# Output products of the MoE stage issued in groups, with four gated blocks kept

## The chip, the cores and the metric

One Trainium2 chip, one of its cores. The metric is device time in microseconds (us), lower is better: the median of several executions of one launch. The core has a matrix engine (TensorE, PE in the rows), with its own row for weight loads (PEld), a vector engine (DVE), an activation engine (ACT), a general engine (POOL) and a queue engine that issues most transfers (SP). PSUM is the memory that TensorE writes to; it has eight banks here, one per accumulator.

## The reference, cut to what matters

```python
# q, k, v: 8 batches x 8 heads x 576 rows x 64 columns
k_p = k.reshape(B, H, 72, 8, D).mean(axis=3)      # v_p likewise
attn = softmax(q @ k_p.T / sqrt(D))               # 72 pooled keys
x = (attn @ v_p), heads joined                    # 4608 tokens x 512
a = x @ w1;  b = x @ w2                           # 512 x 1024 each
out = ((a * b) @ w3) @ w_out                      # 4608 x 512
```

## The kernel before

All numbers are float32, and every large product is made in three passes: a value is split into a rounded part and a rest (`hi`, `lo`), and hi*hi, hi*lo and lo*hi are added in PSUM. The kernel first makes W = w3 @ w_out once (lines 639 to 650). The tokens then go through in 12 chunks (m = 0 to 11) of 384. For a chunk, the 1024 gated columns are eight blocks (j = 0 to 7) of 128, and for each block:

- `a_mm m j` and `b_mm m j` (line 562): twelve matmuls each, 384 columns wide, into PSUM bank `a` and into PSUM bank `b`. There is one bank of each.
- `a_post` (line 572, ACT) copies bank `a` to SBUF; `g_mul` (line 580, DVE) multiplies it with bank `b`. So the next `a_mm` waits for `a_post`, and the next `b_mm` for `g_mul`.
- `g_hi` (line 585, ACT) and `g_lo` (line 591, DVE) split the gated block into `gh` and `gl`. There are two buffers of each.
- `out_mm m j` (line 607): nine matmuls, 512 columns wide, that add the block's share to the banks `o0`, `o1` and `o2`. After the eighth block of a chunk, `out_post` copies these out and SP stores them.

Beside this the attention of a later chunk n is made: `tr_q` (DVE), `s_mm` (line 434, the scores, in four banks of which one is bank `a` up to chunk 6 and bank `b` from 7 on), `soft_max`, `soft_sub`, `soft_exp`, `soft_sum`, `soft2` (lines 446 to 478, mostly DVE), `pt_turn` (line 510, DVE, into the one tile `T`), `pt_move` (line 517, four transfers on SP, out of `T`), `av_mm` (line 535, which uses bank `a` too), `x_hi` and `x_lo` (lines 543 and 546). `pt_turn` of the next part waits until `pt_move` has emptied `T`. POOL sums the pooled keys and values in trees of three adds (lines 381 to 386).

What each engine does next is written out by hand in the string `ORDER`: each engine takes its instructions in that order and none overtakes another on its engine. The entries `at(...)` only make the list of steps that `ORDER` names. The 12 entries of `out_mm` per chunk need only stand behind their `g_lo`, and before the chunk's `out_post`.

Of the kernel before, what the change touches and what calls it, by code (L numbers as in the profile page):

```python
# [19 lines left out]
def kernel(  # L20
# [768 lines left out]
    for m in range(NCH):  # L789
        m0 = M0 + 3 * NJ * m  # L790
        for j in range(NJ):
            k = m0 + 3 * j
# [4 lines left out]
            at("P", k + 2, g_hi, m, j)
            at("P", k + 2.5, g_lo, m, j)
            at("M", k + 5 + ([1.5, 0.0][j] if m >= JOINT - 1 and j < 2 else 0), out_mm, m, j)
        if m < NCH - 1:  # L800
            for t in range(3):
                at("P", m0 + 3 * NJ + 3, out_post, m, t)
    for n in range(1, NCH):
# [4 lines left out]
        else:  # L808
            av = k + (16 if n < JOINT - 1 else 7.5 if n < JOINT else 4.4)
            k -= 0 if n < JOINT - 1 else {JOINT - 1: 5, JOINT: 13}.get(n, 17.5)  # L810
# [8 lines left out]
    for b in range(1, B):  # L819
# [89 lines left out]
        a_post 1 0; g_mul 1 0; prep_k 2 0; prep_k 2 2; out_mm 0 7; out_post 0 0; g_hi 1 0; soft_exp 2 0 1;
        load_q 3 (3,); a_mm 1 1; a_post 1 1; prep_k 2 3; out_post 0 2; soft_max 2 1 1 1; b_mm 1 1; tr_q 3 0;  # L910
        soft_sum 2 0 0; soft_sub 2 1 1 1; load_q 3 (2,); soft_sum 2 0 1; soft2 2 0; a_mm 1 2; pt_turn 2 0;
        g_mul 1 1; g_lo 1 0; out_post 0 1; b_mm 1 2; prep_v 2 0; warm 0; prep_k 2 1; out_mm 1 0;
        soft_sub 2 1 0 1; soft_exp 2 1 0; a_post 1 2; a_mm 1 3; soft_max 2 2 0 0; soft_sub 2 2 0 0; g_hi 1 1;
        g_lo 1 1; pt_move 2 0; soft_sum 2 1 0; out_mm 1 1; soft_max 2 1 1 0; b_mm 1 3; soft_exp 2 2 0;
        soft_sub 2 1 1 0; soft_exp 2 1 1; a_post 1 3; soft_sum 2 1 1; soft2 2 1; pt_turn 2 1; g_mul 1 2;
        a_mm 1 4; g_hi 1 2; g_lo 1 2; b_mm 1 4; soft_max 2 2 1 0; soft_sub 2 2 1 0; soft_exp 2 2 1; pt_move 2 1;
        load_q 3 (1,); out_mm 1 2; prep_k 3 0; soft_sum 2 2 0; g_mul 1 3; load_k 3 3; a_mm 1 5; soft_sum 2 2 1;
        tr_q 3 3; soft2 2 2; prep_k 3 3; load_v 2 1; tr_q 3 1; pt_turn 2 2; g_hi 1 3; g_lo 1 3; a_post 1 4;
        pt_move 2 2; kt_mm 2; tr_q 3 2; load_v 2 2; kt_post 2; g_mul 1 4; b_mm 1 5; a_post 1 5; av_mm 2;
        x_hi 2 0; x_lo 2 0; g_mul 1 5; out_mm 1 3; load_q 4 (0,); x_hi 2 1; x_hi 2 2; x_hi 2 3; g_hi 1 5;  # L920
        g_lo 1 5; a_mm 1 6; x_lo 2 1; b_mm 1 6; g_hi 1 4; x_lo 2 2; a_post 1 6; load_q 4 (3,); g_lo 1 4;
        s_mm 3 (0,1,2); out_mm 1 5; a_mm 1 7; a_post 1 7; b_mm 1 7; x_lo 2 3; load_k 3 2; out_mm 1 4;
        soft_max 3 0 0 0; soft_max 3 1 0 0; soft_sub 3 0 0 0; soft_exp 3 0 0; soft_sub 3 1 0 0; a_mm 2 0;
        load_k 3 1; soft_max 3 1 1 0; soft_sub 3 1 1 0; soft_max 3 0 1 0; soft_sub 3 0 1 0; g_mul 1 6; g_hi 1 6;
        soft_exp 3 0 1; tr_q 4 0; soft_sum 3 0 0; load_q 4 (1,); soft_max 3 1 1 1; soft_sub 3 1 1 1;
        soft_exp 3 1 1; soft_max 3 2 0 0; prep_v 2 1; g_mul 1 7; g_hi 1 7; soft_sum 3 0 1; soft2 3 0;
        load_v 3 1; pt_turn 3 0; g_lo 1 6; soft_max 3 1 0 1; a_post 2 0; soft_max 3 2 1 0; soft_sub 3 1 0 1;
        b_mm 2 0; soft_exp 3 1 0; soft_sum 3 1 0; soft_sum 3 1 1; soft2 3 1; prep_k 3 2; soft_sub 3 2 0 0;
        soft_exp 3 2 0; pt_move 3 0; a_mm 2 1; out_mm 1 6; g_lo 1 7; out_mm 1 7; g_mul 2 0; g_hi 2 0;
        pt_turn 3 1; out_post 1 0; soft_sub 3 2 1 0; g_lo 2 0; a_mm 2 2; out_post 1 1; soft_sum 3 2 0; b_mm 2 2;  # L930
        prep_k 3 1; a_post 2 1; kt_mm 3; out_mm 2 0; a_post 2 2; g_mul 2 2; out_post 1 2; prep_v 2 2;
        pt_move 3 1; g_hi 2 2; g_lo 2 2; out_mm 2 2; b_mm 2 1; a_mm 2 3; kt_post 3; tr_q 4 3; g_mul 2 1;
        b_mm 2 3; g_hi 2 1; g_lo 2 1; tr_q 4 1; move_v 2 0; soft_exp 3 2 1; soft_sum 3 2 1; soft2 3 2;
        a_post 2 3; g_mul 2 3; g_hi 2 3; a_mm 2 4; g_lo 2 3; a_post 2 4; b_mm 2 4; a_mm 2 5; move_v 2 1;
        out_mm 2 1; pt_turn 3 2; pt_move 3 2; av_mm 3; a_post 2 5; g_mul 2 4; x_hi 3 0; x_lo 3 0; x_hi 3 3;
        x_lo 3 3; load_q 4 (2,); tr_q 4 2; g_hi 2 4; x_hi 3 1; b_mm 2 5; g_mul 2 5; x_hi 3 2; g_lo 2 4;
        a_mm 2 6; x_lo 3 1; out_mm 2 3; s_mm 4 (0,1,2); x_lo 3 2; soft_max 4 0 0 0; load_v 3 0; a_post 2 6;
        g_hi 2 5; g_lo 2 5; b_mm 2 6; g_mul 2 6; soft_max 4 1 0 0; soft_sub 4 1 0 0; prep_v 3 0;
        soft_max 4 1 1 0; soft_sub 4 1 1 0; soft_sub 4 0 0 0; soft_exp 4 0 0; soft_sum 4 0 0; soft_max 4 0 1 0;
        soft_sub 4 0 1 0; soft_exp 4 0 1; out_mm 2 5; out_mm 2 4; soft_max 4 1 0 1; soft_sum 4 0 1; soft2 4 0;  # L940
        a_mm 2 7; soft_max 4 2 0 0; pt_turn 4 0; soft_sub 4 2 0 0; prep_v 3 1; b_mm 2 7; soft_max 4 1 1 1;
        warm 9; g_hi 2 6; soft_sub 4 1 0 1; a_post 2 7; g_mul 2 7; g_lo 2 6; soft_max 4 2 1 0; soft_sub 4 2 1 0;
        soft_exp 4 2 1; soft_exp 4 1 0; soft_sum 4 1 0; load_v 3 2; a_mm 3 0; soft_sub 4 1 1 1; soft_exp 4 1 1;
        load_q 5 (0,); tr_q 5 0; b_mm 3 0; g_hi 2 7; g_lo 2 7; out_mm 2 6; load_q 5 (2,); a_post 3 0; g_mul 3 0;
        a_mm 3 1; soft_exp 4 2 0; load_q 5 (3,); a_post 3 1; g_hi 3 0; g_lo 3 0; out_mm 2 7; out_post 2 0;
        out_post 2 1; out_post 2 2; b_mm 3 1; g_mul 3 1; g_hi 3 1; g_lo 3 1; a_mm 3 2; b_mm 3 2; prep_v 3 2;
        soft_sum 4 1 1; soft2 4 1; soft_sum 4 2 0; load_q 5 (1,); soft_sum 4 2 1; a_post 3 2; soft2 4 2;
        g_mul 3 2; a_mm 3 3; a_post 3 3; g_hi 3 2; pt_turn 4 1; pt_move 4 0; pt_turn 4 2; load_k 4 0; b_mm 3 3;
        pt_move 4 1; g_mul 3 3; a_mm 3 4; g_hi 3 3; a_post 3 4; out_mm 3 0; out_mm 3 1; b_mm 3 4; tr_q 5 2;
        a_mm 3 5; load_k 4 1; b_mm 3 5; g_lo 3 2; a_post 3 5; g_lo 3 3; pt_move 4 2; g_mul 3 4; g_hi 3 4;  # L950
        out_mm 3 3; out_mm 3 2; g_mul 3 5; g_hi 3 5; tr_q 5 1; tr_q 5 3; g_lo 3 5; move_v 3 1; prep_k 4 0;
        g_lo 3 4; load_q 6 (0,); move_v 3 0; load_q 6 (2,); av_mm 4; x_hi 4 0; out_mm 3 4; x_lo 4 0; x_hi 4 1;
        x_lo 4 1; x_hi 4 2; x_lo 4 2; x_hi 4 3; x_lo 4 3; s_mm 5 (0,1,2); soft_max 5 0 0 0; soft_max 5 1 0 0;
        soft_max 5 0 1 0; soft_sub 5 0 1 0; soft_exp 5 0 1; soft_max 5 1 1 0; b_mm 3 6; soft_sub 5 1 0 0;
        soft_sub 5 0 0 0; soft_exp 5 0 0; load_k 4 2; a_mm 3 6; soft_sum 5 0 0; tr_q 6 0; load_q 6 (3,);
        a_post 3 6; soft_sum 5 0 1; soft2 5 0; g_mul 3 6; g_hi 3 6; pt_turn 5 0; pt_move 5 0; out_mm 3 5;
        a_mm 3 7; soft_max 5 1 1 1; g_lo 3 6; soft_sub 5 1 1 1; load_k 4 3; soft_sub 5 1 1 0; a_post 3 7;
        soft_max 5 2 0 0; soft_max 5 2 1 0; soft_sub 5 2 1 0; soft_sub 5 2 0 0; b_mm 3 7; soft_exp 5 1 1;
# [154 lines left out]
```

## Time and profile before

| | us |
|---|---|
| median of 3 runs | 732.49 (731.98 to 732.7) |
| the profiled execution, device time | 732.49 |
| its span in the profile | 730.7 |
| TensorE busy (matmul rows) | 716.2 |
| TensorE weight loads busy | 649.7 |
| DVE / ACT / POOL busy | 404.3 / 223.2 / 187.7 |

The profile is one execution. Its span is 1.8 us shorter than the device time of that execution; what lies outside it is start and end of the launch. A row of the time-ordered view gives the start, the time that a run of equal instructions took, the engine, the source line, the operation, the output and the inputs, the count, and in brackets how long the engine had been idle and what released it. Matmuls of one run overlap, so the time from one product to the next is read from start to start.

### The profile page before, as it was taken

To read this page: it belongs to the slowest core of one execution; us is meant where nothing else is said; L and a number is where in the kernel's file an instruction comes from. 1 tells how busy PE (TensorE), PEld (TensorE's weight loads), DVE (VectorE), ACT (ScalarE), POOL (GpSimd) and SP (SyncE) were. 2 spreads that over 40 slices of the span, in tenths; PEclk is the share of its full clock that TensorE was granted. 3 is DMA by queue.
4 is the path that set the end of the run, shared out by engine and by line. 5 is a ranking of instruction groups with operands and counts; after the bars stand their busy time and mean duration, and the time that the engine had idled before them with its cause. 6 is when DMAs were issued, how large, how long until landed. Compare 5 with 4: busy or idle time off the path is not lost.

```text
span 730.7 us, 13679 instructions
## 1 busy us (share of the span) xinstructions
PE 716.2 (98%) x5450; PEld 649.7 (89%) x5450; DVE 404.3 (55%) x789; ACT 223.2 (31%) x503; POOL 187.7 (26%) x243
## 2 busy tenths in 40 slices
...
GB/s 336 321 249 275 245 174 90 115 116 107 85 39 84 71 86 62 115 96 114 72 144 36 111 119 50 95 67 80 115 79 23 65 23 44 30 15 1 44 0 44
DMA packets 117391, 73.78 MB, mean 101 GB/s; under 512 B 76496, under 2 KB 94416, under 8 KB 117328
## 3 DMA queue, kind: packets, MB, share of 16 engines
...
q10 hardware_dynamic: 144, 0.13, 0.1%
...
## 4 chain that ended last, share of the span: by engine, by line
PE 91%; DMA 3%; DVE 2%; POOL 1%; ACT 1%; SPq 1%; issue 1%; DVEq 0%; POOLq 0%
PE b L562 27%; PE a L562 27%; PE o L607 27%; PE a L535 2%; DMA st<-in_k_dram 2%; PE att L434 2%; PE o L639 2%; PE b L639 1%; DMA raw<-in_moe_w_dram 1%; DVE wt L159 1%; DMA PT<-T 0%; POOL st L381 0%; PE a L434 0%; PE b L434 0%; PE att L188 0%
## 5 line engine op out<-in xcount | busy, mean ns | idle before, releaser
L562 PE MATMUL b<-xT,hl 128*128 128x384 f32 x1152 | 217.2, 336 | 0.2 <-DVE a L580 0.2
L562 PE MATMUL a<-xT,hl 128*128 128x384 f32 x1152 | 217.2, 336 | 0.0
L562 PEld LDWEIGHTS a<-xT,hl 128*128 128x128 f32 x1152 | 202.0, 188 | 4.7 <-issue 0.8
L562 PEld LDWEIGHTS b<-xT,hl 128*128 128x128 f32 x1152 | 201.9, 188 | 4.3 <-DVE a L580 0.6
L607 PE MATMUL o<-Wc,gh 128*128 128x512 f32 (+1 forms) x576 | 178.9, 392 | 0.0
L580 DVE TENSOR_TENSOR a<-b,a 128x384 f32<-128x384 f32 x96 | 53.0, 552 | 152.6 <-PE b L562 139.5
L381 POOL TENSOR_TENSOR st<-st 96x512 f32<-96x512 f32 (+3 forms) x52 | 68.1, 1309 | 267.6 <-DMA st<-in_k_dram 147.6
L607 PEld LDWEIGHTS o<-Wc,gh 128*128 128x128 f32 x576 | 106.7, 189 | 20.0 <-issue 1.8
L607 PE MATMUL o<-Wc,gl 128*128 128x512 f32 (+1 forms) x288 | 113.1, 393 | 0.0
L585 ACT CAST gh<-a 128x384 fp32r<-128x384 f32 x96 | 49.0, 513 | 202.1 <-DVE a L580 128.7
L591 DVE TENSOR_TENSOR gl<-a,gh 128x384 fp32r<-128x384 f32 x96 | 62.6, 656 | 72.8 <-ACT gh L585 72.4
L572 ACT COPY a<-a 128x384 f32<-128x384 f32 x91 | 43.5, 478 | 174.6 <-PE a L562 168.3
L607 PEld LDWEIGHTS o<-Wc,gl 128*128 128x128 f32 x288 | 54.1, 188 | 12.2
L510 DVE STREAM_TRANSPOSE T<-EB 128x768 f32<-128x768 f32 x33 | 51.2, 1553 | 12.9 <-DMA PT<-T 12.6
L459 ACT ACTIVATE EB<-EB 128x288 f32<-128x288 f32 x66 | 28.4, 443 | 56.2 <-DVE EB L451 56.0
L382 POOL TENSOR_TENSOR st<-st 96x256 f32<-96x256 f32 (+3 forms) x52 | 40.4, 777 | 4.1
L639 PE MATMUL o<-hl 128*128 128x512 f32 x144 | 41.0, 413 | 0.0
L471 DVE TENSOR_REDUCE sm<-EB 128x4 f32<-128x288 f32 x66 | 28.2, 442 | 10.1 <-ACT EB L459 9.6
L399 POOL DMA_DIRECT2D vm<-vp x64 | 32.4, 514 | 2.6 <-POOL vp L386 2.3
L639 PEld LDWEIGHTS o<-hl 128*128 128x128 f32 x144 | 26.0, 192 | 5.7 <-ACT hl L193 0.6
L478 DVE TENSOR_TENSOR EB<-EB,sm 128x576 f32<-128x576 f32 x36 | 29.2, 812 | 1.2
L446 DVE TENSOR_REDUCE mx<-att 128x4 f32<-128x288 f32 (+2 forms) x72 | 27.7, 395 | 4.0 <-PE att L434 4.0
...
## 6 DMA issues: line engine op xcount, KB each, us to landing
...
```

Of the source, the lines that this page charges most:

```text
L381: nc.gpsimd.tensor_tensor(out=t[:, :, 0:4], in0=t[:, :, 0:4], in1=t[:, :, 4:8], op=ALU.add)
L382: nc.gpsimd.tensor_tensor(out=t[:, :, 0:2], in0=t[:, :, 0:2], in1=t[:, :, 2:4], op=ALU.add)
L399: nc.gpsimd.dma_start(out=vm[b % 2][32 * g:32 * g + KW, c], in_=vp[b][KW * i:KW * i + KW, s])
L478: nc.vector.tensor_tensor(out=E, in0=E, in1=sm.unsqueeze(2).unsqueeze(3).broadcast_to([P, H, KS, KW]), op=ALU.mult)
L510: nc.vector.transpose(out=T.rearrange("p g u i -> p u g i"), in_=Et[n, t][:, :NU * P].rearrange("p (u j g) -> p u g j", u=NU, g=4))
L562: nc.tensor.matmul(out=o, lhsT=w12[j - j % 2 + kt // 2, w][sw][:, c:c + P], rhs=x[sx][:, kt], start=(i == 0), stop=(i == 3 * NK - 1))
L572: (nc.vector.tensor_copy if (m, j) in A_DVE else nc.scalar.copy)(out=a, in_=stage.pop(("a", m, j))[:, :CH])
L580: nc.vector.tensor_tensor(out=g, in0=ps[:, :CH], in1=g, op=ALU.mult)
L585: nc.scalar.copy(out=gh, in_=g)
L591: nc.vector.tensor_tensor(out=gl, in0=g, in1=f(gh), op=ALU.subtract)
L607: nc.tensor.matmul(out=oacc[m][t][x][:, cols], lhsT=(gh, gl)[sg][:, c], rhs=W[j][sw][:, cols], start=(k == 1 and i == 0), stop=(k == NJ an ...
L639: nc.tensor.matmul(out=wacc[h][it], lhsT=w3t[s][sa][:, x * P:(x + 1) * P], rhs=wo[j][sb], start=n == 1, stop=n == 3 * NJ)
```

## The change

From chunk 3 on (`GROUPED = 3`) the due times of the list put the a and b products of four blocks behind each other and then the four output products. Blocks 2, 3, 6 and 7 of a chunk get places of their own for `gh` and `gl` in one SBUF tile (`g_tile`), so that up to four gated blocks can wait for their output product; blocks 0, 1, 4 and 5 use the two buffers of before. `ORDER` is written anew from the end of chunk 0 on, for all engines: matmuls, vector and activation work, and the transfers on SP and POOL. The same steps stand in it; nothing is added or left out. PSUM banks are as before.

```diff
-    JOINT = 6
+    JOINT, GROUPED = 6, 3
...
+    def g_tile(m, j, x):
+        if m < GROUPED or j % 4 < 2:
+            return p2.tile([P, CH], F32R, tag="gh" if x == 0 else "gl", name="g")
+        if "g" not in stage:
+            stage["g"] = p1.tile([P, 4, CH], F32R, tag="PTx", name="g")
+        return stage["g"][:, 2 * (j % 2) + x]
...
-        gh = p2.tile([P, CH], F32R, tag="gh", name="gh")
+        gh = g_tile(m, j, 0)
...
-        gl = p2.tile([P, CH], F32R, tag="gl", name="gl")
+        gl = g_tile(m, j, 1)
...
-            k = m0 + 3 * j
+            k = m0 + 3 * j - (j % 4 if m >= GROUPED else 0)
...
-            at("M", k + 5 + ([1.5, 0.0][j] if m >= JOINT - 1 and j < 2 else 0), out_mm, m, j)
+            at("M", k + 5 if m < GROUPED else m0 + 12 * (j // 4) + 8 + j % 4, out_mm, m, j)
```

The matmul steps of chunk 4 and 5 in the order of before, and in the new one (other engines' steps between them left out; the scores, `av_mm` and `kt_mm` are of later chunks):

```text
before: a4.0 O3.6 b4.0 O3.7 a4.1 b4.1 a4.2 b4.2 AV5 O4.0 O4.1 a4.3 KT4 b4.3 S6 O4.2 a4.4 b4.4 a4.5 O4.3
        b4.5 a4.6 b4.6 a4.7 O4.5 b4.7 O4.4 a5.1 O4.6 a5.0 b5.0 O4.7 b5.1 KT5 AV6 S7 a5.2 O5.0 b5.2 a5.3
new:    a4.0 O3.7 b4.0 a4.1 b4.1 a4.2 b4.2 a4.3 b4.3 AV5 O4.0 KT4 O4.1 S6 O4.2 O4.3 a4.4 b4.4 a4.5 b4.5
        a4.6 b4.6 O4.5 a4.7 b4.7 a5.0 b5.0 O4.4 O4.6 O4.7 a5.1 b5.1 a5.2 KT5 b5.2 AV6 S7 a5.3 b5.3 a5.4
```

Four places of the new `ORDER` with all engines' steps, of which the prediction speaks (chunk 1, 4, 5 and 6):

```text
b_mm 1 2; warm 0; prep_k 2 1; a_mm 1 3; soft_max 2 2 0 0; pt_move 2 0; soft_sub 2 2 0 0; g_hi 1 1; out_mm 1 0;
soft_sub 2 1 0 1; soft_exp 2 1 0; a_post 1 2; g_lo 1 1; out_mm 1 1; ... b_mm 1 3; soft_exp 2 2 0; a_post 1 3;
soft_sum 2 1 1; soft2 2 1; pt_turn 2 1; g_mul 1 2;
...
soft2 6 0; pt_turn 6 0; soft_sub 6 2 0 0; a_mm 4 5; a_post 4 5; pt_move 6 0; g_mul 4 4; b_mm 4 5;
a_mm 4 6; soft2 6 1; g_hi 4 4; g_lo 4 4; load_k 5 3; load_q 7 (0,); load_k 5 0; pt_turn 6 1; a_post 4 6;
g_mul 4 5; soft_max 6 2 1 0; prep_v 4 1; b_mm 4 6;
...
av_mm 6; g_lo 5 1; x_hi 6 0; tr_q 7 3; tr_q 7 2; s_mm 7 (0,1,2); soft_max 7 0 0 0; load_v 5 1; prep_v 5 1;
x_lo 6 0; soft_max 7 1 0 0; ... a_mm 5 3;
...
s_mm 8 (0,1,2); soft_max 8 1 0 0; soft_max 8 1 1 1; x_hi 7 2; soft_sub 8 1 0 0; soft_max 8 1 1 0;
soft_sub 8 1 1 0; soft_sub 8 1 1 1; soft_max 8 0 0 0; soft_sub 8 0 0 0; a_mm 6 3; ... b_mm 6 3;
```

## Rows read from the trace of the kernel before

**Rows 1.** The page, part 1: busy time, share of the span, instructions.
```profile
PE 716.2 (98%) x5450; PEld 649.7 (89%) x5450; DVE 404.3 (55%) x789; ACT 223.2 (31%) x503; POOL 187.7 (26%) x243
```

**Rows 2.** Busy time by stretch, chunks 1 to 11: PE, PEld, DVE, ACT, POOL, clock, DMA.
```profile
130.00:727.00 597.00, 596.48 (x4513) 548.24 (x4504) 301.46 (x606) 137.91 (x307) 125.02 (x165) 1.00 0.29 71
```

**Rows 3.** Waits of PE in the whole span: us in total, times, longest.
```profile
PE att L188 <- DVE Wc L159: 8.9, 2, 8.4
PE att L355 <- POOL km L386: 1.4, 2, 1.1
PE b L562 <- DVE a L580: 0.2, 1, 0.2
```

**Rows 4.** Time-ordered view of PE, 655 to 668 us.
```profile
655.36 0.62 PE L607 MATMUL o<-Wc,gh 128*128 128x512 f32 x2
...
657.44 2.27 PE L562 MATMUL b<-xT,hl 128*128 128x384 f32 x12
659.55 2.24 PE L562 MATMUL a<-xT,hl 128*128 128x384 f32 x12
661.63 0.62 PE L607 MATMUL o<-Wc,gh 128*128 128x512 f32 x2
...
663.72 2.27 PE L562 MATMUL a<-xT,hl 128*128 128x384 f32 x12
665.83 2.24 PE L562 MATMUL b<-xT,hl 128*128 128x384 f32 x12
```

**Rows 5.** Time-ordered view of all engines, 148 to 155 us (chunk 1).
```profile
149.82 0.62 PE L607 MATMUL o<-Wc,gh 128*128 128x512 f32 x2
...
150.24 1.55 DVE L510 STREAM_TRANSPOSE T<-EB 128x768 f32<-128x768 f32 x1 [0.57 <-DMA PT<-T]
...
151.72 0.51 DVE L580 TENSOR_TENSOR a<-b,a 128x384 f32<-128x384 f32 x1
...
152.29 2.37 PE L562 MATMUL b<-xT,hl 128*128 128x384 f32 x12 [0.21 <-DVE a L580]
...
154.49 0.68 PE L562 MATMUL a<-xT,hl 128*128 128x384 f32 x3
```

**Rows 6.** Groups of DVE from 130 us on: count, busy us, mean ns, idle.
```profile
L591 DVE TENSOR_TENSOR gl<-a,gh 128x384 fp32r<-128x384 f32 x89 | 57.6, 651 | 72.6 <-ACT gh L585 72.2
L580 DVE TENSOR_TENSOR a<-b,a 128x384 f32<-128x384 f32 x88 | 48.6, 553 | 147.6 <-PE b L562 134.7 <-issue 7.8 <-ACT a L572 3.6
L510 DVE STREAM_TRANSPOSE T<-EB 128x768 f32<-128x768 f32 x30 | 46.6, 1553 | 12.8 <-DMA PT<-T 12.6
...
L546 DVE TENSOR_TENSOR xT<-a,xT 128x384 fp32r<-128x384 f32 x9 | 5.0, 554 | 21.6 <-ACT xT L543 21.6
```

**Rows 7.** Time-ordered view of PE and DVE, 320 to 324 us (scores of chunk 6).
```profile
320.85 0.27 PE L434 MATMUL a<-kbd,qT 64*64 64x72 f32 x1
...
321.75 0.46 DVE L446 TENSOR_REDUCE mx<-a 128x4 f32<-128x288 f32 x1 [1.25 <-PE a L434]
...
322.49 0.22 DVE L446 TENSOR_REDUCE mx<-a 128x1 f32<-128x72 f32 x1
...
322.51 0.73 PE L607 MATMUL o<-Wc,gh 128*128 128x512 f32 x2
...
323.23 0.45 DVE L451 TENSOR_TENSOR EB<-att,mx 128x288 f32<-128x288 f32 x1
323.60 0.55 DVE L580 TENSOR_TENSOR a<-b,a 128x384 f32<-128x384 f32 x1
...
324.43 0.37 DVE L446 TENSOR_REDUCE mx<-att 128x3 f32<-128x216 f32 x1
```

**Rows 8.** Time-ordered view of DVE and SP, 256 to 265 us (the tile T).
```profile
257.07 1.54 DVE L510 STREAM_TRANSPOSE T<-EB 128x768 f32<-128x768 f32 x1
...
258.64 2.49 SPq L517 DMA_DIRECT2D PT<-T  x4
...
263.13 1.55 DVE L510 STREAM_TRANSPOSE T<-EB 128x768 f32<-128x768 f32 x1 [4.52 <-DMA PT<-T]
```

**Rows 9.** Time-ordered view of DVE and POOL, 345 to 350 us.
```profile
347.40 2.22 DVE L591 TENSOR_TENSOR gl<-a,gh 128x384 fp32r<-128x384 f32 x1
...
347.90 1.30 POOL L381 TENSOR_TENSOR st<-st 72x512 f32<-72x512 f32 x1
...
349.55 0.55 DVE L580 TENSOR_TENSOR a<-b,a 128x384 f32<-128x384 f32 x1
```

**Rows 10.** Time-ordered view of all engines, 724 to 731 us: the last matmuls.
```profile
726.41 0.28 PE L607 MATMUL att<-Wc,gl 128*128 128x256 f32 x1
...
727.18 0.38 ACTq L626 DMA_DIRECT2D out_dram<-ob  x1
```

More of the change, by code (lines that the diff above doesn't have):

```diff
@@ L808 @@
         else:
[L809 to L810 removed]
+            av = k + (16 if n < JOINT - 1 else 7.5 if n < JOINT else 5.4)
+            k -= 0 if n < JOINT - 1 else {JOINT - 1: 5, JOINT: 13}.get(n, 16.5)
             plan_att(n, [k - 2] * NT,
@@ L909 @@
[L909 to L958, printed above, removed]
@@ new lines @@
+        a_mm 1 1; a_post 1 1; out_post 0 2; soft_max 2 1 1 1; b_mm 1 1; tr_q 3 0; soft_sum 2 0 0;
+        soft_sub 2 1 1 1; soft_sum 2 0 1; load_q 3 (2,); soft2 2 0; a_mm 1 2; pt_turn 2 0; load_k 3 3;
+        g_mul 1 1; g_lo 1 0; out_post 0 1; b_mm 1 2; warm 0; prep_k 2 1; a_mm 1 3; soft_max 2 2 0 0;
+        pt_move 2 0; soft_sub 2 2 0 0; g_hi 1 1; out_mm 1 0; soft_sub 2 1 0 1; soft_exp 2 1 0; a_post 1 2;
+        g_lo 1 1; out_mm 1 1; soft_max 2 1 1 0; soft_sub 2 1 1 0; soft_exp 2 1 1; soft_sum 2 1 0; load_k 3 0;
@@ new lines @@
+        prep_k 3 0; b_mm 1 3; soft_exp 2 2 0; a_post 1 3; soft_sum 2 1 1; soft2 2 1; pt_turn 2 1; g_mul 1 2;
+        g_hi 1 2; a_mm 1 4; g_lo 1 2; soft_max 2 2 1 0; b_mm 1 4; soft_sub 2 2 1 0; pt_move 2 1; load_q 3 (1,);
+        out_mm 1 2; soft_sum 2 2 0; soft_exp 2 2 1; g_mul 1 3; soft_sum 2 2 1; tr_q 3 3; soft2 2 2; load_v 2 1;
+        tr_q 3 1; pt_turn 2 2; g_hi 1 3; g_lo 1 3; a_mm 1 5; a_post 1 4; pt_move 2 2; kt_mm 2; tr_q 3 2;
+        kt_post 2; g_mul 1 4; b_mm 1 5; a_post 1 5; g_mul 1 5; g_hi 1 5; av_mm 2; x_hi 2 0; x_hi 2 1; x_hi 2 2;
@@ new lines @@
+        tr_q 4 0; soft_exp 3 0 1; soft_sub 3 1 1 1; a_mm 2 0; load_k 3 2; prep_k 3 2; load_q 4 (2,);
+        soft_exp 3 1 1; soft_sum 3 0 0; load_v 3 0; soft_max 3 1 0 1; soft_sub 3 1 0 1; a_post 2 0;
+        soft_sum 3 0 1; soft2 3 0; g_mul 1 7; soft_max 3 2 0 0; soft_max 3 2 1 0; pt_turn 3 0; pt_move 3 0;
+        g_hi 1 7; g_lo 1 7; out_mm 1 6; soft_sub 3 2 1 0; a_mm 2 1; a_post 2 1; soft_sub 3 2 0 0;
+        soft_exp 3 2 0; prep_k 3 1; soft_exp 3 2 1; b_mm 2 0; g_mul 2 0; g_hi 2 0; out_mm 1 7; out_post 1 1;
```

273 lines of the change are left out of this document (154 added, 119 removed).

## The prediction

> **What bounds the kernel now.** I read the busy shares first. TensorE is busy for 716.2 of 730.7 us, DVE for 404.3, ACT and POOL for less [rows 1]. From 130 us on, when the chunks 1 to 11 run, it is busier still: 596.48 of 597.00 us, at a granted clock of 1.00, the 2.4 GHz level, while DVE works 301.46 us, ACT 137.91 and POOL 125.02 [rows 2]. Then I read who TensorE waits for. There are three entries; 8.9 and 1.4 us of them stand at the lines that make W and the keys of the first batches, and the one that stands in the stretch of the chunks is 0.2 us [rows 3]. So the stretch that the change rewrites has TensorE as its only bound, and a new order can gain in two ways alone: by making the matmuls themselves follow each other faster, or by taking away that one wait. It can lose wherever a matmul comes to stand ahead of something that is not ready.
>
> The speed of the matmuls is read from start to start, in a stretch without waits [rows 4]. An output product lasts 657.44 - 655.36 = 2.08 us, or 663.72 - 661.63 = 2.09. An a or b product lasts 661.63 - 659.55 = 2.08 us behind another one of its kind, but 659.55 - 657.44 = 2.11 and 665.83 - 663.72 = 2.11 right behind an output product. The change from output to a or b thus costs 0.03 us; the other direction costs 0.01 at most. This is the whole price of alternating.
>
> **What grouping can take away.** I count in the two orders how often an a or b product stands right behind an output product: 72 times before, 62 times in the new one. In the listing of chunk 4 and 5 one sees why it is so few: the four output products are due in a row, but the new order still puts a, b or attention steps between most of them; 25 of 96 output products follow another one, against 16 before. Ten changes at 0.03 us are **0.30 us gained**. The score and `av_mm` products are as many as before, and only their neighbours differ; I set their difference at nothing, with the 0.03 us of one changed neighbour as the nearest row, so within 0.1 us either way for the handful that differ.
>
> The wait of 0.2 us is in chunk 1 [rows 5]. `b_mm 1 3` should have followed `out_mm 1 1` after 2.09 us, at 151.91, and began at 152.29, 0.38 later, because `g_mul 1 2` stood on DVE behind a `pt_turn` that waited for its transfer. The product itself then lasted 154.49 - 152.29 = 2.20 instead of 2.08, so the event cost 0.38 + 0.12 = 0.50 us: a matmul stream that had stopped needs 0.12 more to be at its pace. In the new order the same steps stand there: `pt_turn 2 1`, then `g_mul 1 2`, then the need of `b_mm 1 3`, with the same two output products ahead of it. One load more stands ahead on SP, a `soft_sub` less on DVE. Whether the event returns depends on that one transfer, so I take half: **0.25 us gained**, with 0 and 0.50 as ends.
>
> **What the new order adds on TensorE's path.** Products of four blocks in a row mean that `b_mm` of block j+1 has only `a_mm` (2.08 us) between it and `b_mm` of block j, in place of 2.08 + 2.09 us with an output product between. In that time `g_mul` (0.55 us, rows 6) must get its turn on DVE, and what stands ahead of it there decides. I followed the four engines' queues of the new order from one matmul to the next with the durations of rows 6 to 8 and looked for places where the reserve is under the length of one DVE instruction. Elsewhere the reserve is larger. Three places come out short:
>
> - `a_mm 5 3` needs bank `a`, which `av_mm 6` filled and `x_lo 6 0` empties. In the new order `x_lo 6 0` stands on DVE behind `soft_max 7 0 0 0`, which waits for the scores of chunk 7. A reduce of fresh scores starts 321.75 - 320.85 = 0.90 us after the scores begin and takes 0.46; scores take 322.51 - 320.85 = 1.66 [rows 7]; `x_lo` takes 0.55 [rows 6]. DVE instructions on different data overlap by 0.08 (323.23 + 0.45 against 323.60, rows 7). 0.90 + 0.46 + 0.55 - 0.08 = 1.83, some 0.05 for the signal to arrive, against 1.66: short by 0.22 us.
> - `b_mm 6 3` needs bank `b`, which holds scores of chunk 8. It follows scores and one a product: 1.66 + 2.2 = 3.86 us. Ahead of `soft_sub 8 0 0 0`, which empties it, stand six DVE instructions from the last bank of scores on (1.66 us, and 0.21 of lag: the first bank of scores is full after 5 of 12 parts, 0.69 us, and read at 0.90; so 1.87): lengths 0.22, 0.22, 0.37, 0.37, 0.22, 0.46, then 0.45 itself [rows 7], 2.31 together, less 0.3 of overlap. 1.87 + 2.01 + 0.1 = 3.98: short by 0.12 us.
> - `b_mm 4 6` needs `g_mul 4 5`, which stands behind `pt_turn 6 1`, which waits until the transfers of `pt_turn 6 0` have left `T`. `pt_turn` takes 1.55, the four transfers end 263.13 - 258.64 = 4.49 us after the first is issued [rows 8], then `pt_turn` and `g_mul` again: 1.55 + 4.49 + 1.55 + 0.47 = 8.06 us. In the queues `pt_turn 6 0` comes level, some 0.25 us late, with the start of `b_mm 4 4`, and four products lie between: 8.32 us. 8.06 + 0.25 + 0.05 against 8.32: about even, short by up to 0.1 us.
>
> Together 0.22 + 0.12 + 0.05 = 0.39 us of waiting, and each time 0.12 for the restart as in rows 5, 0.36: **0.75 us lost**. Bounds: 0 (the estimates are each within 0.2 us of no wait) and, above, three events of the size of rows 5, 1.5 us.
>
> **What is moved at no cost.** `gh` and `gl` in four places: same instructions, other addresses; their cover is that ACT and DVE have more than 290 us idle in 597 [rows 2]. The transfers are the same; SP's `pt_move` takes 2.49 us to issue [rows 8], and loads now stand in bunches ahead of some (all four `load_q 5` before `pt_move 4 1`), but that one waits for `pt_turn 4 1`, which comes later than they do. POOL's trees keep their order among themselves, and POOL has 472 us of idle time. If that cover were gone, the price is that of the third place. The end does not move: the last step is output block 7 of chunk 11 in both orders, 4.3 us before the end of the span [rows 10].
>
> **Sum**, on the profiled execution: 730.7 - 0.30 - 0.25 + 0.75 = 730.9 us of span, with the 1.8 us around it 732.7 us, that is 0.2 over its own 732.49, which is also the median of the three runs. I call it no change: 0.2% is 1.46 us, about what a measurement of this kernel can tell from none.
>
> **Rivals.**
>
> - *All reserves hold.* The three places are estimates near zero; if none waits and the event of rows 5 is gone: 730.7 - 0.30 - 0.50 = 729.9, 731.7 us in device time. For it speaks that before had places with as little reserve and one wait in 597 us. It is still within 0.2%.
> - *DVE's queue is held by a transfer, and with products in a row TensorE feels it* (slower). The place is `pt_turn` in front of `g_mul`. Before, a hold of 4.52 us [rows 8] passed without a wait, since output products lay ahead of the next b product; a hold of 0.57 in the wrong place cost 0.50 us [rows 5]. There are 30 `pt_turn` with 12.6 us of such holds [rows 6]. If a transfer is a microsecond late at `b_mm 4 6` (1.0 + 0.12) and one more place per three chunks is hit as in rows 5 (three times 0.5), the loss over the forecast is 2.6 less the 0.75 that it holds: 734.5 us. It decides from about three events on.
> - *`g_lo` is stretched by POOL.* `g_lo` took 2.22 us at 347.40 while POOL's add of 1.30 us ran, and `g_mul` came after both [rows 9]; its mean is 651 ns where `g_mul`, of equal size, takes 553 [rows 6], so some 8.7 us in 89. An a product or b product that waits behind such a `g_lo` would lose up to 2.22 - 0.56 = 1.66 us; two of them with the forecast's waits give 732.7 + 2 x 1.66 = 736.0. Against it: the 8.7 us of before cost TensorE nothing, and the output product, which needs `g_lo`, now comes later. The Trainium skill ("SBUF — State Buffer", Who interferes with whom) says that a DVE instruction with two SBUF inputs and a POOL instruction that reads SBUF take one port pair in turn, each for its whole length; the trace agrees with the 2.22 us.
> - *The weight loads have reserve.* They are busy for 548.24 of the 597.00 us [rows 2]. Were the 48.8 us between them a loss that order can win back, a tenth would give 732.5 - 4.9 = 727.6. Rows 4 speak against it: an output product keeps 2.08 to 2.09 us whatever stands before it. The Trainium skill ("Perfetto Trace Analysis", Identifying the Most-Contended Engine) judges TensorE's headroom by the share of its weight loads, not of its matmuls, and would see this 8%.
>
> **Chances.** Forecast, 731.9 to 733.5: 0.57. All reserves hold, 731.4 to 731.9: 0.20. DVE held by a transfer, 733.5 to 735.5: 0.15. POOL's stretch, above 734: 0.05. Weight loads, or anything else that makes it faster than 731.0: 0.03. Slower by over 0.2% means above 733.95: the two slower rivals for the most part, 0.17, and 0.01 of the forecast's tail, 0.18. Faster 0.03, no change 0.79. The range from 731.6 to 734.6 leaves out some 0.1 below and 0.1 above.
>
> **What would show it.** The profile after should have 2.08 and 2.11 us in the same places and ten fewer of the latter; TensorE busy for all but 1 us from 130 us on; waits of PE on `x_lo` (line 546) before `a_mm 5 3`, on `soft_sub` (line 451) before `b_mm 6 3`, on `g_mul` before `b_mm 4 6`, each 0.3 us or less. The forecast is wrong if PE's list shows waits at line 562 of more than 2 us in sum, if `pt_turn` shows far more than 12.6 us of waiting and PE waits with it, or if the products themselves have another length.

## The result, and the profile after

| | before | after |
|---|---|---|
| median, us | 732.5 (731.98 to 732.7, 4 runs) | 738.12 (736.51 to 740.55, 4 runs) |
| ratio, 95% interval | | 1.0071 [1.0052, 1.0091] |
| profiled execution: device time, span | 732.49, 730.7 | 738.11, 736.3 |

The changed kernel is 0.7% slower, and its runs lie further apart. The prediction had said 732.7, no change, within 731.6 to 734.6. Line numbers from 582 on are 7 higher in the kernel after.

The page of the kernel after (its engines, which answer to [rows 1], and one line of the DMA queues: packets, MB, share of 16 engines):

```profile
PE 718.3 (98%) x5450; PEld 650.5 (88%) x5450; DVE 397.5 (54%) x789; ACT 223.2 (30%) x503; POOL 185.7 (25%) x243
...
q8 instruction: 43, 0.70, 0.4%
```

The stretch of [rows 2], in the kernel after:

```profile
130.00:727.00 597.00, 593.77 (x4525) 545.49 (x4524) 295.45 (x608) 136.63 (x305) 125.20 (x168) 1.00 0.29 71
```

The waits of PE after, as in [rows 3] (us in total, times, longest):

```profile
PE a L562 <- issue: 1.3, 1, 1.3
PE att L434 <- issue: 1.0, 1, 1.0
...
PE b L562 <- DVE a L580: 0.6, 1, 0.6
...
PE a L562 <- DVE mx L446: 0.3, 1, 0.3
```

Two of these waits have no releaser: "issue" is time in which the engine waited for nothing that the profile shows. The time-ordered view of PE after shows where all four are:

```profile
340.39 2.36 PE L562 MATMUL b<-xT,hl 128*128 128x384 f32 x12 [0.63 <-DVE a L580]
342.59 2.25 PE L614 MATMUL o<-Wc,g 128*128 128x512 f32 x9
...
372.08 2.35 PE L562 MATMUL a<-xT,hl 128*128 128x384 f32 x12 [0.27 <-DVE mx L446]
...
425.17 1.10 PE L434 MATMUL att<-kbd,qT 64*64 64x72 f32 x57
426.19 1.34 PE L562 MATMUL a<-xT,hl 128*128 128x384 f32 x6
428.85 1.34 PE L562 MATMUL a<-xT,hl 128*128 128x384 f32 x6 [1.32 <-issue]
430.03 2.24 PE L562 MATMUL b<-xT,hl 128*128 128x384 f32 x12
...
589.61 1.08 PE L434 MATMUL att<-kbd,qT 64*64 64x72 f32 x53
591.70 0.34 PE L434 MATMUL att<-kbd,qT 64*64 64x72 f32 x4 [1.00 <-issue]
591.97 2.19 PE L562 MATMUL a<-xT,hl 128*128 128x384 f32 x11
```

The first two rows with a wait are `b_mm 4 6` and `a_mm 5 3`, two of the prediction's three places. The third stop is in the middle of `a_mm 6 3`, behind the scores of chunk 8: six of its matmuls run, then nothing for 1.32 us, then the other six, which read the same kind of data. The fourth is inside the scores of chunk 11, four matmuls before their end. No bank, no data and no engine can be missing there.

Where the time is, from start to start (in the profiled execution of each kernel): `a_mm 1 0` starts at 136.10 us after and at 133.10 before, 3.0 later; from there to the last output product it is 594.01 against 591.31, 2.7 more. Within the chunks, each step's time over the usual time of its kind (2.08, 2.11 and so on, as in [rows 4]) is 0.80 + 0.12 at `b_mm 4 6`, 0.34 at `a_mm 5 3`, 1.64 at `a_mm 6 3`, 1.33 at the scores of chunk 11: 4.23 us. The wait of [rows 5], 0.50 us, is gone. Up to `a_mm 1 0`, TensorE's own order is the same in both kernels.

### The profile page after: what moved, and what is told of

Read it like the earlier page. It is cut to its first block, busy times and chain, and to the rows that moved or that the text cites. A ratio compares the mean times of both kernels' runs of the same rounds, so it can differ in the third digit from the quotient of the medians.

```text
span 736.3 us, 13616 instructions
## 1 busy us (share of the span) xinstructions
PE 718.3 (98%) x5450; PEld 650.5 (88%) x5450; DVE 397.5 (54%) x789; ACT 223.2 (30%) x503; POOL 185.7 (25%) x243
## 4 chain that ended last, share of the span: by engine, by line
PE 86%; DMA 7%; ACT 2%; SPq 2%; DVE 1%; issue 1%; POOL 0%; DVEq 0%; ACTq 0%
PE o L614 26%; PE b L562 26%; PE a L562 26%; DMA raw<-in_moe_w_dram 5%; PE a L535 2%; PE att L434 1%; SPq L271 1%; PE o L646 1%; DMA st<-in_k_dram 1%; PE b L434 0%; PE a L434 0%; DMA PT<-T 0%; PE att L188 0%; PE att L614 0%; DVE wt L159 0%
## 5 line engine op out<-in xcount | busy, mean ns | idle before, releaser
L614 PE MATMUL o<-Wc,g 128*128 128x512 f32 (+1 forms) x864 | 210.4, 391 | 0.0
L614 PEld LDWEIGHTS o<-Wc,g 128*128 128x128 f32 x864 | 160.0, 188 | 32.9 <-issue 2.4
L592 ACT CAST g<-a 128x384 fp32r<-128x384 f32 x96 | 48.9, 514 | 143.3 <-DVE a L580 112.9
L598 DVE TENSOR_TENSOR g<-a,g 128x384 fp32r<-128x384 f32 x96 | 56.3, 592 | 50.6 <-ACT g L592 50.2
L282 DVE STREAM_TRANSPOSE qT<-qs 128x384 f32<-128x384 f32 x40 | 22.0, 562 | 9.6 <-DMA qs<-in_q_dram 9.6
L451 DVE TENSOR_TENSOR EB<-att,mx 128x288 f32<-128x288 f32 (+2 forms) x66 | 25.1, 393 | 0.9
```

The lines of the kernel that those rows point to most:

```text
L614: nc.tensor.matmul(out=oacc[m][t][x][:, cols], lhsT=(gh, gl)[sg][:, c], rhs=W[j][sw][:, cols], start=(k == 1 and i == 0), stop=(k == NJ an ...
```

## The experiments

**The idea.** The trace of the kernel after has 11,009 instructions of TensorE: each matmul is two (a weight load and the matmul), the other 109 are nearly all waits. The page lists 43 packets of a queue called instruction, 0.70 MB, so 16 KB each; 11,009 / 43 = 256. And the packets go with TensorE's count: the last six of this trace begin when it is at number 154 to 170 of a block of 256. So TensorE gets its instructions during the run, 256 at a time. "Place" is an instruction's number in the trace, counted from TensorE's first one, modulo 256; where the packets' own limits lie in this count is not shown. Both unexplained stops are at the same place, 194 and 193, as if the instructions at hand ended there until the next packet has come. An AV product and the scores behind it are the fastest stretch in instructions: `av_mm 7` and `s_mm 8` are 386 of them in 3.8 us, where an a or b product has 24 in 2.08. The change puts the a and b products of block 2 ahead of `av_mm 7` and `av_mm 10`, 48 instructions, and no other product comes or goes there; 8 wait instructions fewer stand ahead of the one and 18 fewer ahead of the other. So `av_mm 7` starts at place 52 (12 before), `av_mm 10` at 70 (40 before).

The DMA view of the kernel after for 424.0 to 425.7 us, and then for 425.7 to 427.7 (queue: packets, MB, share of 16 engines), around the third stop:

```profile
q1 hardware_dynamic: 413, 0.47, 103.6%
...
q1 hardware_dynamic: 2146, 0.30, 104.5%
q8 instruction: 1, 0.02, 4.9%
```

The scores pass place 256 (0 of the next block, a mark for comparison) at about 424.6 us; the packet of instructions begins only at 426.03, while the ordinary queue keeps the DMA engines full, and TensorE goes on at 428.85. At the scores of chunk 11 a packet begins at 589.31 with no other transfer under way, and TensorE goes on at 591.70, 2.4 us later.

All kernels below are timed against the kernel before on the same chip; "chunks 1 to 11" is from the start of `a_mm 1 0` to that of the last output product, in the profiled execution.

**Chance at the start: both kernels again.** No edit.

> The kernel before once more, unchanged, to see what varies from run to run. Theory A (the 3.0 us that the changed kernel is behind when chunk 1 starts are chance of that one execution: TensorE's clock rose at 15.9 instead of 13.5 us, transfers landed later): this run's first product of chunk 1 starts anywhere between 132 and 137 us (133.1 in the first trace), and the time spreads by a microsecond or more. Theory B (they belong to the changed kernel): 133.1 us within 0.5, time 732.5 within 0.5.

> The changed kernel once more, unchanged. Theory A: first product of chunk 1 anywhere between 132 and 137 us; Theory B: 136.1 within 0.5 again. From chunk 1 on both expect the same four gaps as in the first trace: about 0.8 us ahead of the b product of block 6 of chunk 4, 0.3 at the a product of block 3 of chunk 5, 1.3 to 1.6 around the scores of chunk 8 and 1.3 inside the scores of chunk 11; time 736.5 to 740.5.

Before again: 732.68 us (731.57 to 734.16), ratio 0.9999 [0.999, 1.0009]; `a_mm 1 0` at 132.60; chunks 1 to 11 590.88. After again: 737.56, 1.0075 [1.0055, 1.0095]; `a_mm 1 0` at 133.44; 594.32. So the loss in the chunks comes again (1.14 + 0.12, 0.34, 2.24 and 0.75 over the usual times), and the 3.0 us at the start don't. The waits without a releaser in this second profile of the kernel after:

```profile
PE a L562 <- issue: 1.9, 1, 1.9
...
PE att L434 <- issue: 0.4, 1, 0.4
```

Over all 16 profiles of this study `a_mm 1 0` starts between 132.15 and 136.10, in the order of before between 132.60 and 134.85. That part is chance.

**The same order, other places.**

```diff
     def warm(i):
+        if i == 4:
+            ps = patt.tile([P, 512], F32, tag="att", name="att")
+            for _ in range(104):
+                nc.tensor.matmul(out=ps[:32, :32], lhsT=ident[:, :32], rhs=ident[:, :32], start=True, stop=True)
```

> The changed kernel with 104 tiny matmuls (32 columns, 32 rows out, a result nobody reads) put in front of TensorE's first work, where it stands idle for 8.4 us anyway. Nothing else moves; every later TensorE instruction stands 208 places further on in TensorE's instruction stream. Theory C (the two gaps of 1.3 to 1.6 us at the scores of chunks 8 and 11 are TensorE running out of instructions: 16 KB of them, 256 instructions, are loaded at a time, and the fast stretch of AV product and scores, some 390 instructions in 3.8 us, reaches the end of what is loaded 2.4 to 2.8 us after the next load began): both gaps go, no new one over 0.3 us comes, and chunks 1 to 11 take 591.0 us instead of 594.0; time about 3 us under the changed kernel's on this chip. Theory D (the gaps are waits of the new order that the profile can't name, for a bank, a transfer or another engine): both stay within 0.3 us of 1.3 to 1.6, time as the changed kernel.

Each of these matmuls ran as two, so the shift was 416 and not 208: `av_mm 7` at place 211, `av_mm 10` at 229. Measured: 732.29 us, ratio to before 0.9996 [0.9984, 1.0009]; chunks 1 to 11 take 590.85, as expected, 3.5 under the changed kernel's second profile. Between the medians it is 5.3 us, more than the 3 expected; the 1.8 beside the chunks are not explained by a profile. PE has no wait on "issue" any more, and what is left shows the prediction's own three places (time-ordered view of PE; a and b of block 6 of chunk 4, then block 3 of chunk 6):

```profile
334.33 2.25 PE L566 MATMUL a<-xT,hl 128*128 128x384 f32 x12
336.49 2.35 PE L566 MATMUL b<-xT,hl 128*128 128x384 f32 x12
338.68 0.62 PE L618 MATMUL o<-Wc,g 128*128 128x512 f32 x2
...
422.27 2.38 PE L566 MATMUL a<-xT,hl 128*128 128x384 f32 x12
424.65 2.34 PE L566 MATMUL b<-xT,hl 128*128 128x384 f32 x12
426.83 1.37 PE L566 MATMUL a<-xT,hl 128*128 128x384 f32 x7
```

The excess is 0.08 + 0.11 (2.16 and 2.19), 0.34 at `a_mm 5 3`, and 0.20 + 0.10 (2.38 and 2.18): 0.83 us.

The kernel before, shifted into the bad places (24 tiny matmuls):

> The kernel before with 24 of the same tiny matmuls in TensorE's idle time at the start: 48 places further on. That brings the AV product of chunk 7 to place 59 and that of chunk 10 to place 87 of a 256-instruction block (12 and 40 before; 52 and 70 in the changed kernel, where the gaps are). Theory C: the kernel before gets the gaps too, about 1.0 to 1.6 us at the scores of chunk 8 and 1.0 to 1.5 at those of chunk 11, and chunks 1 to 11 take 593.3 to 594.3 us instead of 591.3; time 734.3 to 735.5. Theory D: no gap, 732.5 within 0.5.

The shift was 96 and not 48: `av_mm 7` at 107, `av_mm 10` at 135, other places than the expectation reckons with, which turned out bad too. 734.55 us, ratio 1.0031 [1.0018, 1.0044]; chunks 1 to 11 593.78, 2.9 more than before's 590.88. Its time-ordered view of PE, with the two stops, again at place 194 each:

```profile
417.12 0.83 PE L438 MATMUL att<-kbd,qT 64*64 64x72 f32 x35
418.96 0.60 PE L438 MATMUL att<-kbd,qT 64*64 64x72 f32 x22 [1.01 <-issue]
...
581.85 0.58 PE L438 MATMUL att<-kbd,qT 64*64 64x72 f32 x21
583.06 0.84 PE L438 MATMUL att<-kbd,qT 64*64 64x72 f32 x36 [0.63 <-issue]
```

The control, a shift by one whole block (64 tiny matmuls):

> Control for the tiny matmuls: the changed kernel with 64 of them (128 on the chip, 256 places: one whole block, so that every place within a block is as in the changed kernel, less one). Theory C: the gaps at the scores of chunks 8 and 11 are back at the same places (7 matmuls into the next a product, and 4 before the end of the scores), 1.3 to 2.3 and 0.7 to 1.3 us; time as the changed kernel within 1 us. Theory F (it was the tiny matmuls' work in the idle time, through the clock or the start of the transfers, that gave the time back, not the places): no gaps, time 732.3.

737.71 us, ratio 1.0063 [1.004, 1.0086]; stops of 1.98 and 0.75 at places 193 and 194. Time-ordered view of PE:

```profile
424.97 1.31 PE L566 MATMUL a<-xT,hl 128*128 128x384 f32 x6
428.10 1.20 PE L566 MATMUL a<-xT,hl 128*128 128x384 f32 x6 [1.82 <-issue]
```

So the tiny matmuls neither help nor harm by their work; the place decides. Theories D (waits of the order that the profile can't name) and F (the tiny matmuls' own work) fall.

**The buffers alone.** The kernel before, own order, with `GROUPED = 3` and `g_tile` from the change.

> The kernel before, in its own order, with the four kept places for gated blocks added (the new tile and its use, nothing else): the buffers without the new order. Theory C (instruction loads) and the prediction's waits both put the loss on the order: 732.5 to 733.2, no gap over 0.5 us from chunk 1 on. Theory E (the new tile itself costs: another place in SBUF, longer first steps of chunk 0): first product of chunk 1 later than 133.5 us, time over 734.5.

733.04 us, 0.9995 [0.9984, 1.0006]; chunks 1 to 11 590.20, no stop over 0.15. The new tile does not cost. It even gives some 0.6 us of the chunks: see the last section.

**The prediction's places mended, alone and with the shift.**

```diff
-... s_mm 7 (0,1,2); soft_max 7 0 0 0; load_v 5 1; prep_v 5 1; x_lo 6 0; ...
+... s_mm 7 (0,1,2); x_lo 6 0; soft_max 7 0 0 0; load_v 5 1; prep_v 5 1; ...
-... pt_turn 6 1; a_post 4 6; g_mul 4 5; ...
+... g_mul 4 5; pt_turn 6 1; a_post 4 6; ...
-... s_mm 8 (0,1,2); soft_max 8 1 0 0; ... soft_max 8 0 0 0; soft_sub 8 0 0 0; a_mm 6 3; ...
+... s_mm 8 (0,1,2); soft_max 8 0 0 0; soft_sub 8 0 0 0; soft_max 8 1 0 0; ... a_mm 6 3; ...
```

> The changed kernel with the prediction's three places mended in the order alone: the read of bank a of chunk 6's first part ahead of the first maximum of chunk 7, the maximum and subtraction that empty bank b first after the scores of chunk 8, the product with bank b of block 5 of chunk 4 ahead of the transpose that waits for the transfers. TensorE's own order is untouched. Theory C: the gaps ahead of b of block 6 of chunk 4 (0.9 to 1.3 with its restart) and a of block 3 of chunk 5 (0.34) go, both gaps at the scores of chunks 8 and 11 stay (1.3 to 2.3 and 0.7 to 1.3): time 1.2 to 1.6 us under the changed kernel, about 736. The rival (all four gaps are waits of the order): the gap at the scores of chunk 8 goes too, 734.

738.24 us, 1.006 [1.0041, 1.008], not 736: a miss. The places mended are gone from the profile as expected, and both stops on instructions stay, but the one at `a_mm 6 3` was 2.53 us here, and it had a second price (time-ordered view of PE, then busy time by stretch, where the third column from the end is the granted clock):

```profile
427.97 1.27 PE L562 MATMUL a<-xT,hl 128*128 128x384 f32 x6 [2.34 <-issue]
...
429.04 3.79 PE L562 MATMUL b<-xT,hl 128*128 128x384 f32 x12
432.66 1.56 PE L562 MATMUL a<-xT,hl 128*128 128x384 f32 x8
```

```profile
426.00:428.00 2.00, 0.03 (x1) 0.03 (x1) 1.53 (x4) 0.00 (x0) 0.00 (x0) 1.00 0.40 63
428.00:429.00 1.00, 1.00 (x6) 1.00 (x6) 0.00 (x0) 0.00 (x0) 0.00 (x0) 0.99 0.74 144
429.00:430.00 1.00, 1.00 (x6) 1.00 (x4) 0.00 (x0) 0.66 (x2) 0.00 (x0) 0.50 0.99 251
...
432.00:433.00 1.00, 1.00 (x6) 1.00 (x5) 0.07 (x1) 0.00 (x0) 0.84 (x3) 0.81 0.55 89
433.00:434.00 1.00, 1.00 (x8) 1.00 (x7) 1.00 (x3) 0.00 (x0) 1.00 (x2) 1.00 0.25 39
```

TensorE was idle for 2.3 us, worked again from 427.97 on, and at 428.97 its clock went from 1.00 to 0.50, the 1.2 GHz level, for 3.41 us; the b product took 1.54 us longer. The Trainium skill ("TensorE: Matmul & The Clock Gate", What's actually happening) says that the slow clock is the default and that activity releases it. These rows agree in that the clock rose again to 1.00 under unbroken work. In the kernel after, stops of 1.3 and 1.9 us at the same matmuls left the clock at 1.00. Of the executions of the kernels that stop at the scores of chunk 8, the changed kernel's first four included, 13 of 29 have a mean clock of 0.998 or less; of all those of the kernel before, none, and of those of the other kernels in the new order 2 of 72. That is probably a part of why the changed kernel's runs lie apart.

> Both at once: the three places mended and the 104 tiny matmuls in front (each came out as two matmuls on the chip, so 416 places: 160 past a block). Theory C: nothing of the four gaps is left; chunks 1 to 11 take 590.1 (590.85 with the tiny matmuls alone, less 0.2 + 0.34 + 0.3 of the three places); time 731.5, 0.7 under the one with the tiny matmuls alone, the fastest so far.

731.34 us (730.6 to 732.8), ratio 0.9979 [0.9969, 0.9989]: faster than both kernels, if by little. Chunks 1 to 11 take 590.29, of which 0.43 us are two small waits; the stretch of [rows 2] is full but for 0.25 us:

```profile
130.00:727.00 597.00, 596.75 (x4549) 548.69 (x4547) 293.97 (x607) 137.41 (x307) 123.07 (x166) 1.00 0.29 71
```

**One part undone.** Chunk 6 is shown, chunk 9 is alike (scores of chunk 11). The maximum and subtraction that empty bank `b` (`soft_max 8 0 0 0`, `soft_sub 8 0 0 0`) also come first after the scores here, which mends the prediction's third place.

```diff
-... a_mm 6 2; a_post 6 2; b_mm 6 2; g_mul 6 2; g_hi 6 2; av_mm 7; ... s_mm 8 (0,1,2); ... a_mm 6 3; ... b_mm 6 3;
+... av_mm 7; ... s_mm 8 (0,1,2); ... a_mm 6 2; a_post 6 2; b_mm 6 2; a_mm 6 3; ... g_mul 6 2; g_hi 6 2; b_mm 6 3;
```

> The changed kernel, no added matmuls, with one part of the new order undone in chunks 6 and 9 alone: the a and b products of block 2 go back behind the scores of chunks 8 and 11 (with their copies and products on the other engines), as they stood before. That puts the AV products of chunks 7 and 10 two products, 48 places, earlier: at 4 and 22 of a block (52 and 70 in the changed kernel). Theory C (instruction loads): the gaps at the scores of chunks 8 and 11 go, the two other gaps (0.9 to 1.3 in chunk 4, 0.34 in chunk 5) stay; chunks 1 to 11 take 591.5; time 733.0 within 0.6. Rival (the gaps come from the fast stretch itself, wherever it lies, or from the products of later blocks): they stay or move, time over 735.

736.28 us, 1.0046 [1.0025, 1.0067]. Both stops on instructions are gone, as the theory says, but 733 was missed: `av_mm 7` uses the output banks, now comes a product pair earlier, and waits for their copies, 1.79 us with what follows. With the two other places mended too, and then with the vector engine's copy moved up:

> The products back as in the run above, and the two other places of the prediction mended (chunk 4's product ahead of the waiting transpose, chunk 5's read of bank a ahead of the maximum): no added matmuls. All four gaps go: chunks 1 to 11 take 590.3, time 731.5 within 0.6, as with tiny matmuls and mended places, and about 1.2 us under the kernel before.

> As the run with the products back and the waits mended, but with the vector engine's copy of the second output bank of chunk 5 put right behind the first one's, ahead of a transpose and of the subtraction and product of chunk 6. If the 1.79 us ahead of AV product 7 were that copy's lateness, they go: chunks 1 to 11 take 589.9 (591.63 less 1.75), time 731.8 within 0.5. If not (no spare in the stretch), a gap of over 0.8 us stays there or goes to the next product, time 733.

733.59 us, 1.0008 [0.9998, 1.0018], and 734.03, 1.0017 [1.0004, 1.0031]: the first missed its 731.5 by the same wait (chunks 1 to 11 take 591.63, not 590.3), and the copy gains nothing. The wait at `av_mm 7` (time-ordered view of PE of the one and of the other) only changed its releaser, from the vector engine's copy to the activation engine's, which stands behind `g_hi 6 1` and so behind `b_mm 6 1`:

```profile
417.10 0.80 PE L535 MATMUL o<-PT,vm 32*64 32x192 f32 x3 [0.84 <-DVE ob L630]
```

```profile
417.40 0.37 PE L535 MATMUL o<-PT,vm 32*64 32x192 f32 x1 [1.27 <-ACT ob L632]
```

So this way of mending costs a wait of its own, which perhaps the move of both copies would take away; that was not tried.

**At the edge of the bad places** (24 tiny matmuls in the changed kernel).

> The changed kernel with 24 tiny matmuls in front (48 on the chip, 96 places): the AV product of chunk 7 starts at 147, that of chunk 10 at 165 of a block. Theory C, at an edge: the scores of chunk 8 reach place 193 of the block about 1.9 us after the load began, where 2.4 to 2.8 are wanted, so a smaller gap of 0.3 to 1.0 us in the middle of the scores of chunk 8; none at chunk 11, where the load begins while TensorE still works on the b product ahead of the AV product. Theory G (an instruction load of 16 KB that falls among the transfers out of the transposed tile makes the wait in chunk 4 longer: 0.08 + 0.11 us without, 0.80 to 1.14 + 0.12 with): here none falls there, so that gap is 0.1 to 0.4 with its restart. Chunks 1 to 11 about 591.9, time 732.5 to 734.

736.71 us, 1.0049 [1.0032, 1.0065], not 732.5 to 734: a miss. No stop at chunk 11, as expected, and chunk 4's wait down to 0.17 + 0.11. But the stop in the scores of chunk 8 was far larger than 0.3 to 1.0:

```profile
420.56 0.47 PE L438 MATMUL att<-kbd,qT 64*64 64x72 f32 x15
424.40 1.60 PE L438 MATMUL att<-kbd,qT 64*64 64x72 f32 x42 [3.38 <-issue]
425.93 4.13 PE L566 MATMUL a<-xT,hl 128*128 128x384 f32 x12
```

The packet began 2.8 us after place 256 was passed, and the clock fell at 423.00, 2.0 us into the stop, for 6.83 us (the row 425.93: twelve matmuls in 4.0 us instead of 2.1). Busy time by stretch, with the clock in the third column from the end:

```profile
423.00:425.00 2.00, 0.60 (x21) 0.59 (x24) 0.00 (x0) 0.00 (x0) 0.00 (x0) 0.50 0.43 66
```

What I had left out of the estimate are the transfers behind which the packet waits. In the five profiles of the new order that stop at chunk 8, loads of q keep the DMA engines full there and the packet begins 1.4 to 2.8 us after place 256; in the five that stop at chunk 11 no other transfer runs there, and it begins 0.1 to 0.7 us after.

**The transfers ahead of the packet** (in the changed kernel, places untouched).

```diff
-load_v 6 0; load_q 9 (0,); load_q 9 (2,); load_k 6 1; load_q 9 (1,); load_q 9 (3,); ... pt_move 8 0;
+pt_move 8 0; load_v 6 0; load_q 9 (0,); load_q 9 (2,); load_q 9 (1,); load_q 9 (3,); load_k 6 1;
```

> The changed kernel with its places untouched; the loads of q for chunk 9, of a third of v and of two k pieces are put behind the first transfer out of the tile of chunk 8, so that few transfers are under way when the scores of chunk 8 run. Theory H (the instruction load at these scores begins 1.1 to 1.4 us late and takes up to 1.6 us because it stands in line with those transfers): its gap falls from 1.6 to 2.5 us to 1.0 to 1.3, as at chunk 11 where no transfer runs; time 0.5 to 1.2 us under the changed kernel. Rival (the gap is set by the place alone): it stays at 1.6 to 2.5.

734.82 us, 1.0026 [1.0012, 1.004]. The stop at chunk 8 is gone, more than expected; only the wait on bank `b` is left (2.38, as with the tiny matmuls). The packet began at 423.4, ahead of the scores (423.5) and of place 256 (423.6). Time-ordered view of PE, and DMA share (last column but one) of the AV product and scores, first of the changed kernel, then of this one:

```profile
424.15 1.10 PE L434 MATMUL att<-kbd,qT 64*64 64x72 f32 x57
425.18 2.38 PE L562 MATMUL a<-xT,hl 128*128 128x384 f32 x12
427.56 2.35 PE L562 MATMUL b<-xT,hl 128*128 128x384 f32 x12
```

```profile
422.00:426.00 4.00, 4.00 (x191) 3.47 (x193) 1.72 (x4) 1.76 (x4) 1.65 (x2) 1.00 0.93 251
```

```profile
421.00:425.00 4.00, 4.00 (x191) 3.47 (x193) 1.72 (x4) 1.76 (x4) 1.82 (x2) 1.00 0.21 70
```

So at chunk 8 it takes both, the place and the transfers ahead of the packet; at chunk 11, with no transfer under way, the place alone is enough (0.87 here).

> The changed kernel with the loads of chunk 9 late (as above, place 51 of the block for AV product 7 unchanged), the products of block 2 back behind the scores in chunk 9 alone, and the three predicted places mended; no added matmuls. If place and transfers in line must come together for the gap at chunk 8, and place alone makes the one at chunk 11: no gap over 0.3 us but the one of chunk 1 (0 to 0.9, which comes and goes); chunks 1 to 11 take 590.0 to 590.9, time 731.9 within 0.6. If the place alone is enough at chunk 8 too: a gap of 1 us or more there in some executions, time 733 or more.

732.4 us (730.93 to 734.86), ratio 0.9996 [0.9983, 1.0008]; chunks 1 to 11 take 589.85, and no step is more than 0.06 us over its usual time. Why its median is 1.1 us over that of the kernel with tiny matmuls, with a shorter stretch in the profile, stays open; the start up to `a_mm 1 0` varies by more than that.

The places and stops together:

```text
kernel                          av_mm 7  stop at chunk 8   av_mm 10  stop at chunk 11
products back (3 kernels)            4   none                   22   none
before (2), its buffers alone       12   none                   40   none
changed (2)                         52   1.64, 2.24             70   1.33, 0.75
changed, places mended              51   2.53 + 1.54 clock      69   1.38
changed + 256                       51   1.98                   69   0.75
changed, loads late                 52   none                   70   0.87
loads late, chunk 9 back            51   none                   21   none
before + 96                        107   1.34                  135   0.96
changed + 96                       147   4.35 + 1.78 clock     165   none
changed + 416 (2)                  211   none                  229   none
```

Kernels that share a row differ by at most 1 in place. Every stop of this table lies at place 193 or 194; why there, no run shows.

## Why the prediction was wrong

**The bound.** Right: TensorE alone, before and after.

**The three places.** Right in place and nearly in size. Where nothing else disturbs, they cost 0.83 us, against 0.75: 0.19 at `b_mm 4 6` (0.17 in the sum), 0.34 at `a_mm 5 3` (0.34), 0.30 at `b_mm 6 3` (0.24). In the changed kernel itself the first is 0.92 and 1.26. There a packet of instructions begins in the middle of the four transfers of `pt_move 6 0`. From their first issue to the start of the transpose that waits for them passed 5.04 to 5.68 us in the five profiles where it does, and 4.38 and 4.48 (4.49 in the sum) in the two where the shift has moved it away (with waits of 0.08 and 0.17). The transfers and the hold of the transpose, in the changed kernel and with the 104 tiny matmuls:

```profile
333.29 2.50 SPq L517 DMA_DIRECT2D PT<-T  x4
...
338.33 1.56 DVE L510 STREAM_TRANSPOSE T<-EB 128x768 f32<-128x768 f32 x1 [1.16 <-DMA PT<-T]
```

```profile
330.06 2.51 SPq L521 DMA_DIRECT2D PT<-T  x4
...
334.44 1.56 DVE L514 STREAM_TRANSPOSE T<-EB 128x768 f32<-128x768 f32 x1 [0.46 <-DMA PT<-T]
```

**The event of chunk 1.** Half was a fair value: of 12 profiles in the new order five have it, with 0.31 to 0.89 us and some 0.08 for the restart; the changed kernel's two don't. In the profiled execution the whole 0.50 was gained, which is chance.

**The changes from output to a or b.** Right, but only a part of the gain. Without stops, chunks 1 to 11 take 590.8 in the order of before and 589.85 in the new one: 0.95 us, not 0.30. The rest is for the most part in the kept places, which I had set at nothing (last section): with the buffers alone, in the order of before, the chunks take 590.20.

**The step that failed** is the one called "What is moved at no cost", and the sentence of the first paragraph, that the order can lose where a matmul "comes to stand ahead of something that is not ready". I followed banks, data and queues for each moved step, and took TensorE's own instructions for granted. Two products moved ahead of AV product and scores shift their places by 40 and 30, and the load of the next 256 instructions, hidden behind slow products before, came to lie in the fastest stretch: 1.64 + 1.33 us in the first profile, 2.24 + 0.75 in the second, and in some executions, as their mean clocks suggest, the clock's fall on top. The kernel before is free of these stops by its places alone: shifted by 96 places it has them. The SP loads "in bunches" were followed to the transfers that wait behind them, not to the packet of instructions that waits behind them. With 0.75 more at `b_mm 4 6` the forecast would have been 732.7 + 2.97 + 0.75 = 736.4; the median is 738.12. In the profiled execution (738.11) the late start, 3.0 us, with 0.25 less for the event of chunk 1 and 0.65 less for the kept places, makes 738.5, near enough. In the median the clock and the start may explain a part; there is no profile of the slower executions, and this remainder stays open.

**The rivals.** "All reserves hold" is false as long as the places are not mended. DVE's queue did feel a transfer, at the place named, but one such place, not one in three chunks. POOL's stretch did not come: `g_lo` has a mean of 577 ns from 130 us on, 651 before [rows 6]. The weight loads' reserve was not won: 545.49 us busy after, 548.24 before [rows 2], and the products behind each other keep their 2.08 us. The line set for being wrong, over 2 us of PE waits at line 562, was passed; that the longest of them would be called "issue" I had not thought of.
